# Three edits to a routed attention and bilinear feed-forward kernel: no arithmetic on GpSimd, one PSUM bank of their own for the preparations, sorting scratch in another weight's room

## The chip, the cores and the metric

One core of a Trainium2 chip runs the whole program. The metric is the device time of one execution in microseconds (us); the kernel before was timed three times, and its median is compared. The core has five engines that run their own instruction streams in order and wait for each other by semaphores: PE (TensorE, matrix products), DVE (VectorE), ACT (ScalarE), POOL (GpSimd) and SP (SyncE, which here only starts transfers).

## The reference

```python
# attention: q, k, v are (4 batches, 8 heads, 768 tokens, 64), 16 centroids per head
q_n = q / (norm(q) + 1e-06);  k_n, c_n likewise
q_assign = argmax(einsum('bhsd,hcd->bhsc', q_n, c_n), axis=-1)   # one of 16 clusters
k_assign = argmax(einsum('bhsd,hcd->bhsc', k_n, c_n), axis=-1)
mask = q_assign[:, :, :, None] == k_assign[:, :, None, :]
scores = where(mask, matmul(q, k^T) / 8, -1e9)
attn = softmax(scores);  out = matmul(attn, v)
# feed-forward on x = out as (3072 tokens, 512)
a = x @ w_a;  b = x @ w_b            # 512 -> 1536, float64 inputs, used as float32
y = (a * b) @ w_out                  # 1536 -> 512
```

## The kernel before, in words

**Two ways to do the attention.** Heads are taken in pairs, four pairs to a batch, 16 in all. The first eight pairs (batches 0 and 1) are *dense*: all 768x768 scores of a head are computed, and a one-hot code of the cluster, added as a small bf16 product before the real one (`score`, L590, both), makes a key of another cluster vanish in the exponential. The other eight pairs (numbers n = 1 to 8, batches 2 and 3) are *sorted*: rows of q, k and v are scattered by indirect transfers into lists by cluster (`put`, L1410), each list is reloaded and attended by itself (L1482 to L1526), and results are gathered back (`get`, L1547) and transposed (L1562).

**The dense loop.** It runs over 48 groups of two key blocks. In each group PE computes scores (L590), ACT takes the exponential (L600), PE multiplies the probabilities by v (`weigh`, L636), and DVE adds probabilities up for the softmax denominator (`add_up`, L619; for the first pair POOL does it, L624). Once per half pair PE sums over keys (`denominators`, L655), ACT copies that out (L660), and DVE transposes, inverts and scales (`normalize`, L675 to L689; the scaling of pairs 0 to 2 is POOL's). Between these stand the *preparations* of the next dense pair: for pairs 4 to 7 a transpose on DVE (L503), similarities to the centroids on PE (`prep_sim`, L400), a transpose back (L507), the choice of the best cluster (L528 to L533), the one-hot code (L513, L515), its transpose (L519), and eight small transfers that spread it (L523). The sorted pairs' first steps are preparations too: transposes of the rows (L1249, copied out at L1254), similarities (L1260), and positions in the lists (L1307, L1309).

**The weights.** 36 parts of 128x512 float64 words arrive by transfers into two buffers named `raw` (L299) and are turned into float32 by `round_w`: four instructions on DVE (L310, L313, L317, L320), two on ACT, and a last add of the rest on POOL (L328). Parts 0 to 23 are `w_a` and `w_b`, parts 24 to 35 `w_out`, one for each block of 128 of the 1536 middle features. Eight have fixed places in the dense loop; the others are put in by a planner that runs in Python while the program is written. It keeps a clock of its own for each engine (`Clocked`) and a list of events with due times. It decides only the order: what the chip runs is a fixed list for each engine.

**The feed-forward.** Batch 0 is done in two token halves, each of 24 *pieces* of eight matmuls (`ffn_block`: `piece_a` with `w_a`, copied out by ACT; `piece_b` with `w_b`, multiplied into `h` by DVE, L774). 12 of them fall into the dense loop, one in about two groups. Batches 1 to 3 and all second products (`ffn_downs`) use Strassen's scheme of seven products for eight; DVE makes the differences of operands first (L1004 of `h`, L993 of `w_out`, L820 of x) and adds the products up (L1027). All products of the feed-forward share L715.

**PSUM and SBUF.** PSUM has two double banks for scores (`ps_s`), three single banks (`ps_m`) and one for the attention output (`ps_o`). Before the feed-forward begins, preparations take `ps_m`; from then on the feed-forward owns all three banks in turn (`in_turn`), and `apart()` gives a preparation one of the score tiles. The rows of sorted pairs 1 to 4 wait in the room of `h` of the second token half, their keys and scratch in the room of the first (`early_room`). So the fifth piece of the first half has to come after the last positions of pair 4 (`"after", EARLY`), and the second half's pieces after its last scatter (`"put", EARLY`). `late_room` opens new rooms after that.

Of the kernel before, what the change touches and what calls it, by code (L numbers as in the profile page):

```python
# [11 lines left out]
FP32 = mybir.dt.float32  # L12
# [5 lines left out]
ALU = mybir.AluOpType  # L18
# [139 lines left out]
def short_path(nc, tc, ctx, c, cn, centroids_in, casts, n_far, q, k, v,  # L158
# [22 lines left out]
    G_, Gi = (Clocked(nc.gpsimd, "G", us, *state) for us in (1.1, 1.28))  # L181
# [120 lines left out]
    def round_w(i):  # L302
# [25 lines left out]
        G_.tensor_tensor(out=w, in0=w, in1=rest, op=ALU.add)  # L328
# [282 lines left out]
    def add_up(u):  # L611
        p, hf, j = where(u)
        if j == 0 or j == NJ - 1:
            return
        if j == 1:
            accs[p, hf] = accp.tile([P, 2, HB], FP32, name="acc")
        acc = accs[p, hf]
        if p > 0:
            Vd.tensor_tensor(out=acc, in0=probs[u - 1] if j == 1 else acc,  # L619
                             in1=probs[u], op=ALU.add)  # L620
            added[p, hf] = clocks["V"]
            return
        for a in range(2):
            G_.tensor_tensor(  # L624
                out=acc[:, a, :],
                in0=probs[u - 1][:, a, :] if j == 1 else acc[:, a, :],
                in1=probs[u][:, a, :], op=ALU.add)
        added[p, hf] = clocks["G"]
# [35 lines left out]
    def normalize(p, hf):  # L664
# [21 lines left out]
        def apply():  # L686

            eng = V if p >= HP - 1 else G_
            eng.tensor_tensor(out=x, in0=x, in1=den, op=ALU.mult)  # L689
            unchecked.append((4 * p + 2 * hf + 1, inv))  # L690
# [53 lines left out]
    def ffn_block(b, blk):  # L744
# [14 lines left out]
        def piece_a(f):  # L759
            while blk == 0 and f == NCH and ("after", EARLY) not in done:  # L760
                spend(1.0)
                run_due()
            if f == 0:
                while blk == 1 and ("put", EARLY) not in done:
                    spend(1.0)
                    run_due()
                box["h"] = early[blk].rearrange("p (f t) -> p f t", f=NF)
# [375 lines left out]
    wanted, issued = {}, [0.0]  # L1143
# [80 lines left out]
    def sorted_pair(n, start):  # L1224
# [398 lines left out]
        def run_chain(chain, first=0.0):  # L1623
            at_step = [0]

            def step(t):
# [5 lines left out]
                if not gate() or late and clocks[kind] > now[0] + late or (  # L1632
# [8 lines left out]
                f()  # L1641
                at_step[0] += 1
# [14 lines left out]
    blocks, left = {}, {}  # L1657
# [17 lines left out]
    def ffn_ready(p, hf):  # L1675
# [8 lines left out]
        if hf == 0:  # L1684
            blocks[0] = ffn_block(0, 0)
            ffn.extend(counted(0, blocks[0][0]))
        else:
            ups0, box0 = blocks[0]
            ups, box = ffn_block(0, 1)
            pieces = ups  # L1690
# [17 lines left out]
    PER_GROUP = NCH * HB // 2  # L1708
# [25 lines left out]

    def next_round(t):
# [9 lines left out]
        at(t + 6.0, next_round)  # L1745
# [116 lines left out]
    check_inverses()  # L1862
    while events or len(ffn) > 10:
# [283 lines left out]
```

## Time and profile before

| what | value |
|---|---|
| median of 3 runs (lowest, highest) | 1027.24 us (1027.18, 1029.36) |
| the profiled execution's own time | 1026.05 us |
| its span, first to last instruction | 1024.3 us |
| mean granted TensorE clock | 0.981 |
| PE busy | 973.9 us |
| DVE busy | 612.3 us |
| ACT busy | 281.5 us |
| POOL busy | 375.3 us |

The span is what the trace covers; 1.75 us of the profiled execution lie around it. The dense loop ends near 309 us; from there PE runs the feed-forward with the sorted pairs between its pieces. A busy time is the union of an engine's instructions; the granted clock is the share of full speed at which PE was allowed to run, and a matmul at half of it takes twice as long.

### The profile page before, as it was taken

To read this page: it belongs to the slowest core of one execution; us is meant where nothing else is said; L and a number is where in the kernel's file an instruction comes from. 1 tells how busy PE (TensorE), PEld (TensorE's weight loads), DVE (VectorE), ACT (ScalarE), POOL (GpSimd) and SP (SyncE) were. 2 spreads that over 40 slices of the span, in tenths; PEclk is the share of its full clock that TensorE was granted. 3 is DMA by queue.
4 is the path that set the end of the run, shared out by engine and by line. 5 is a ranking of instruction groups with operands and counts; after the bars stand their busy time and mean duration, and the time that the engine had idled before them with its cause. 6 is when DMAs were issued, how large, how long until landed. Compare 5 with 4: busy or idle time off the path is not lost.

```text
span 1024.3 us, 20493 instructions
## 1 busy us (share of the span) xinstructions
PE 973.9 (95%) x7966; PEld 508.1 (50%) x7966; DVE 612.3 (60%) x1256; ACT 281.5 (27%) x586; POOL 375.3 (37%) x359
## 2 busy tenths in 40 slices
PE   8988958898799999999999999999999999999997
PEld 5443323343344454665554556755454665444564
DVE  5599869779665574767765653755353534333442
ACT  5755635353453331101222210112122001111100
POOL 3515856445564213434454443344443310000000
PEclk9999989999899999999999999999999999999999
DMA  6987455532236654564746277272832302222300
GB/s 184 240 228 164 108 122 151 124 92 79 77 100 169 157 103 100 157 148 108 133 105 150 71 167 184 66 174 82 166 83 66 124 27 73 56 59 62 119 32 30
DMA packets 266776, 118.86 MB, mean 116 GB/s; under 512 B 197552, under 2 KB 252848, under 8 KB 266672
## 3 DMA queue, kind: packets, MB, share of 16 engines
q1 hardware_dynamic: 257040, 104.44, 41.3%
q0 software_dynamic: 9216, 12.60, 4.5%
q8 instruction: 65, 1.06, 0.4%
q10 hardware_dynamic: 416, 0.43, 0.1%
q14 instruction: 39, 0.32, 0.1%
HBM read 79.46 MB, written 37.55 MB: 114 GB/s over the span
## 4 chain that ended last, share of the span: by engine, by line
PE 73%; DVE 3%; SPq 1%; DMA 1%; ACT 1%; issue 1%; DVEq 0%
PE m L715 62%; PE s L590 2%; PE s L1482 2%; PE O L636 2%; PE s L1507 2%; PE s L1516 1%; DMA raw<-down_sums 1%; PE O L1249 1%; PE s L1562 1%; PE s L655 0%; SPq L523 0%; PE O L1260 0%; SPq L1238 0%; SPq L990 0%; SPq L1440 0%
## 5 line engine op out<-in xcount | busy, mean ns | idle before, releaser
L1547 POOL DMA_INDIRECT xT<-od,idx x96 | 93.8, 977 | 123.1 <-PE m L715 118.0
L715 PE MATMUL m<-xT,wa_sb 128*64 128x384 f32 x672 | 116.5, 487 | 0.0
L715 PE MATMUL m<-xT,wb_sb 128*64 128x384 f32 x672 | 116.2, 487 | 0.0
L600 ACT ACTIVATE pt<-s 128x768 f32<-128x768 f32 x96 | 75.2, 809 | 97.3 <-PE s L590 56.8
L892 DVE TENSOR_TENSOR ha<-ha,m 128x384 f32<-128x384 f32 x72 | 39.7, 552 | 95.0 <-PE m L715 71.9
L889 ACT COPY h<-m 128x384 f32<-128x384 f32 x72 | 34.5, 479 | 199.5 <-PE m L715 180.0
L715 PE MATMUL m<-wo_sb,h 128*64 128x256 f32 x768 | 87.3, 380 | 0.0
L892 DVE TENSOR_TENSOR h<-h,m 128x384 f32<-128x384 f32 x72 | 39.7, 551 | 72.4 <-PE m L715 55.4
L715 PE MATMUL m<-raw 128*64 128x384 f32 x432 | 79.1, 487 | 1.0 <-DVE raw L854 1.0
L636 PE MATMUL O<-pt,v 128*64 128x384 f32 x384 | 75.8, 518 | 3.2 <-ACT xT L643 3.2
L590 PE MATMUL s<-qkT 64*128 64x384 f32 x384 | 77.8, 523 | 0.0
L715 PEld LDWEIGHTS m<-xT,wb_sb 128*64 128x64 f32 x672 | 47.8, 137 | 59.1 <-issue 55.1
L715 PEld LDWEIGHTS m<-xT,wa_sb 128*64 128x64 f32 x672 | 47.4, 137 | 58.4 <-issue 53.3
L1410 POOL DMA_INDIRECT qd<-whole,idx x48 | 48.2, 1005 | 68.3 <-PE m L715 53.9
L1410 POOL DMA_INDIRECT kvd<-whole,idx x48 | 48.7, 1014 | 63.0 <-PE m L715 49.8
L1410 POOL DMA_INDIRECT qd<-h,idx x48 | 54.9, 1143 | 44.3 <-PE O L636 24.2
L715 PEld LDWEIGHTS m<-wo_sb,h 128*64 128x64 f32 x768 | 54.6, 137 | 28.4 <-issue 1.4
L715 PE MATMUL m<-xT,h 128*64 128x256 f32 x576 | 64.9, 380 | 0.0
L1410 POOL DMA_INDIRECT kvd<-h,idx x48 | 51.3, 1070 | 26.9 <-PE s L590 14.6
L590 PE MATMUL s<-ohT 64*128 64x384 bf16 x192 | 30.0, 342 | 28.1 <-DMA ohT<-h 15.6
L715 PE MATMUL m<-xT,size 128*64 128x384 f32 x288 | 52.7, 487 | 0.0
L715 PEld LDWEIGHTS m<-xT,h 128*64 128x64 f32 x576 | 40.7, 137 | 20.8 <-DVE h L1004 0.5
(286 smaller groups left out, 1518.1 us busy)
## 6 DMA issues: line engine op xcount, KB each, us to landing
whole<-kvd SPq DMA_DIRECT2D x64, 160.0 KB
raw<-in_moe_w_a_dram SPq DMA_DIRECT2D x12, 512.0 KB
raw<-in_moe_w_b_dram SPq DMA_DIRECT2D x12, 512.0 KB
raw<-in_moe_w_out_dram SPq DMA_DIRECT2D x12, 512.0 KB
raw<-up_sums SPq DMA_DIRECT2D x96, 64.0 KB
kvd<-xT SPq DMA_DIRECT2D x4, 1280.0 KB
whole<-qd SPq DMA_DIRECT2D x32, 160.0 KB
od<-whole SPq DMA_DIRECT2D x32, 160.0 KB
```

The lines of the kernel that those rows point to most:

```text
L590: ins = nc.tensor.matmul(out=s[:, a, 0:HB], lhsT=Ts[p][r, S + j * P:S + (j + 1) * P], rhs=Ts[p][r, hf * HB:(hf + 1) * HB], start=start, st ...
L600: Sl.activation(out=pt, in_=s[:, :, 0:HB], func=AF.Exp, scale=SCALE)
L636: ins = nc.tensor.matmul(out=O_of[0][a * D:(a + 1) * D, 0:HB], lhsT=vs[p][:, a, j, :], rhs=probs[u][:, a, :], start=(j == 0), stop=(j == N ...
L715: ins = nc.tensor.matmul(out=ps[half], lhsT=lhsT[:, half], rhs=rhs, **kw)
L889: S_.copy(out=box[name], in_=box["X"][:, 0:HB])
L892: V.tensor_tensor(out=box[name], in0=box[name], in1=box[bank][:, 0:HB], op=ALU.add)
L1249: nc.tensor.transpose(out=ps[:, x * P:(x + 1) * P], in_=(M["qr"], M["kk"])[w][:, j].rearrange("p a d -> p (a d)"), identity=ident)
L1410: ins = Gi.indirect_dma_start(out=dst[:, :], out_offset=bass.IndirectOffsetOnAxis(ap=M["idx"][:, w, j, a:a + 1], axis=0), in_=src, in_offs ...
L1482: nc.tensor.matmul(out=tiles[s // 2][r0:r0 + m, s % 2, c0:c0 + m], lhsT=M["skT"][r, h, 32 * x:32 * x + m], rhs=M["sqT"][r, h, 32 * x:32 * ...
L1507: nc.tensor.matmul(out=ps[:, s, 65 * i:65 * i + 65], lhsT=pt[:, P * i:P * i + P], rhs=vt[:, i, :], start=True, stop=True)
L1516: nc.tensor.matmul(out=ps[r, s, 65 * (2 + i):65 * (3 + i)], lhsT=pt[r, 2 * P + D * i:2 * P + D * i + D], rhs=vt[r, 2 + i, :], start=True, ...
L1547: paced(Gi.indirect_dma_start(out=M["xs"][:, j, a * D:(a + 1) * D], out_offset=None, in_=od[n][:, :], in_offset=bass.IndirectOffsetOnAxis( ...
```

## The change

POOL loses its three kinds of adds and multiplies, which become DVE instructions. `in_turn` takes two banks in place of three, and the third one, `beside`, is handed to every preparation until `late_room` gives it back to the feed-forward. A gate spaces the preparations of sorted pairs by 0.3 us of planned time. Rows and scratch of sorted pairs 1 to 4 move from the first half's `h` into the room of `w_out` (one of the two row buffers stays in the second half's `h`). With that the waits of the pieces change, and so does their order: 16 pieces of the first half, the second half's blocks 6, 7 and 0 to 5, the rest of the first half, the rest of the second. `PER_GROUP` rises, which lets 15 pieces fall into the dense loop. The rounding of the weights gets new rules: parts 8 to 15 from a date on or when DVE is idle, 16 to 23 when it is idle, and `w_out` only after the last scatter of pair 4. What is left of the rounding is written in one go before the first product of `ffn_downs` (`with_weights`, unchanged).

```diff
@@ round_w
-        G_.tensor_tensor(out=w, in0=w, in1=rest, op=ALU.add)
+        V.tensor_tensor(out=w, in0=w, in1=rest, op=ALU.add)
@@ apart
-    banks = []
+    banks, beside = [], []
     def apart():
+        if beside:
+            return beside[0]
         if banks:
             return ps_s.tile([P, 2, 512], FP32, name="s")[:, 0, :]
@@ add_up
-        if p > 0:
-            Vd.tensor_tensor(out=acc, in0=probs[u - 1] if j == 1 else acc,
-                             in1=probs[u], op=ALU.add)
-            added[p, hf] = clocks["V"]
-            return
-        for a in range(2):
-            G_.tensor_tensor(
-                out=acc[:, a, :],
...
-        added[p, hf] = clocks["G"]
+        Vd.tensor_tensor(out=acc, in0=probs[u - 1] if j == 1 else acc,
+                         in1=probs[u], op=ALU.add)
+        added[p, hf] = clocks["V"]
@@ normalize
-            eng = V if p >= HP - 1 else G_
-            eng.tensor_tensor(out=x, in0=x, in1=den, op=ALU.mult)
+            V.tensor_tensor(out=x, in0=x, in1=den, op=ALU.mult)
@@ in_turn
-            banks.extend(ps_m.tile([P, 512], FP32, name="m") for _ in range(3))
+            banks.extend(ps_m.tile([P, 512], FP32, name="m") for _ in range(2))
+            beside.append(ps_m.tile([P, 512], FP32, name="m"))
@@ piece_a
-            while blk == 0 and f == NCH and ("after", EARLY) not in done:
+            if blk == 0 and f >= NF - 2:
+                assert dense_done
+            while blk == 1 and f < NF // 2 and ("put", EARLY - 1) not in done:
                 spend(1.0)
                 run_due()
-            if f == 0:
-                while blk == 1 and ("put", EARLY) not in done:
-                    spend(1.0)
-                    run_due()
@@ early_room
-        rooms([t[:, 0:ROW], t[:, ROW:2 * ROW]], extra[:, 2 * S:4 * S],
-              early[0][:, 3 * S:], early[0][:, 2 * S:])
+        w = wo_sb.rearrange("p f n -> p (f n)")
...
+        rooms([new(ROW), t[:, 0:ROW]], new(2 * S), new(HB + 512 + 2 * (NJ + 1) * 2 * NC),
+              new(2 * NJ * D))
@@ late_room
         dense.close()
+        banks.append(beside.pop())
@@ run_chain, step
-                if not gate() or late and clocks[kind] > now[0] + late or (
+                if not gate() or kind == "T" and side_at[0] > now[0] or late and (
+                        clocks[kind] > now[0] + late) or (
...
+                if kind == "T":
+                    side_at[0] = last[0] + 0.3
@@ ffn_ready
-            ffn.extend(counted(0, blocks[0][0]))
+            ffn.extend(counted(0, blocks[0][0][:16]))
...
-            pieces = ups
+            part = lambda fs: [x for f in fs for x in ups[2 * f:2 * f + 2]]
+            pieces = part((6, 7, 0, 1, 2, 3, 4, 5)) + later[16:] + part((8, 9, 10, 11))
@@ the dense loop and the rounding
-    PER_GROUP = NCH * HB // 2
+    PER_GROUP = NCH * HB * 5 // 8
...
+    def may_round(i):
+        idle = clocks["V"] <= now[0] + 0.6
+        if i < 16:
+            return idle or now[0] > ROUND + 9.0 * (i - 8)
+        if i < 24:
+            return idle and now[0] > 240 or ("put", EARLY) in done
+        return idle and was("put", EARLY, 4)
+
+    ROUND = 122.0
...
-        if not (i in raws and arrived[i] + 4.5 <= now[0] and clocks["V"] <= now[0] + 1.0):
+        if not (i in raws and arrived[i] + 4.5 <= now[0] and may_round(i)):
             at(now[0] + 0.5, next_round)
...
-        at(t + 6.0, next_round)
+        at(max(t + 3.5, now[0]), next_round)
```

More of the change, by code (lines that the diff above doesn't have):

```diff
@@ L1142, in short_path @@
     busy = []
-    wanted, issued = {}, [0.0]
+    wanted, issued, side_at = {}, [0.0], [0.0]
     ROW = 2 * NJ * 3 * D
@@ L1176, in early_room, with new @@
         early.append(t)
-        rooms([t[:, 0:ROW], t[:, ROW:2 * ROW]], extra[:, 2 * S:4 * S],
-              early[0][:, 3 * S:], early[0][:, 2 * S:])
+        w = wo_sb.rearrange("p f n -> p (f n)")
+        at_ = [0]
+        def new(n):
+            at_[0] += n
+            return w[:, at_[0] - n:at_[0]]
+        rooms([new(ROW), t[:, 0:ROW]], new(2 * S), new(HB + 512 + 2 * (NJ + 1) * 2 * NC),
+              new(2 * NJ * D))
     def late_room():
         dense.close()
+        banks.append(beside.pop())
         post = ctx.enter_context(tc.tile_pool(name="post", bufs=1))
@@ L1655, in n_stat @@
         return slice(c0, c0 + 1)
-    blocks, left = {}, {}
+    blocks, left, dense_done = {}, {}, []
     def counted(b, pieces):
```

9 lines of the change are left out of this document (4 added, 5 removed).

## The prediction

> **What bounds the kernel now.** I read the page first, then the busy times by stage, then what PE waits for in the stages where it idles.
>
> ```profile
> span 1024.3 us, 20493 instructions
> ```
> ```profile
> 52.00:134.00 82.00, 67.60 (x444) 30.93 (x440) 73.02 (x131) 44.56 (x86) 44.57 (x33) 0.95 0.63 154
> 134.00:140.00 6.00, 1.12 (x6) 0.73 (x8) 4.16 (x7) 0.00 (x0) 2.10 (x2) 0.50 0.15 44
> 140.00:265.00 125.00, 108.56 (x644) 46.91 (x642) 102.67 (x176) 56.17 (x109) 67.78 (x59) 0.94 0.48 115
> 265.00:309.00 44.00, 41.41 (x239) 18.59 (x241) 27.37 (x45) 22.39 (x47) 27.80 (x25) 0.92 0.33 106
> 309.00:407.00 98.00, 98.00 (x775) 46.63 (x773) 54.86 (x109) 28.24 (x63) 25.43 (x24) 1.00 0.62 134
> 407.00:1024.00 617.00, 608.83 (x5525) 338.51 (x5521) 321.62 (x722) 97.40 (x223) 183.38 (x185) 1.00 0.40 102
> ```
>
> The windows give, after the length, the busy time of PE, PEld, DVE, ACT and POOL, then the granted clock. From 309 us on PE idles 8.2 us in 715: that part is bound by PE, and the change leaves PE its products. So what can be won lies in the dense loop: 14.4 us idle in 52 to 134, 4.9 in the next 6, and 16.4 + 2.6 = 19.0 from 140 to 309. What can be lost is a new gap after 309. DVE is nearly as full as PE in the loop: 73.02 of 82.
>
> The table of waits for PE, 140 to 309 us, names the owner of those 19.0:
>
> ```profile
> PE s L590 <- ACT acc L660: 5.8, 8, 2.1
> PE s L590 <- DMA ohT<-h: 4.2, 4, 2.1
> PE s L590 <- ACT xT L1254: 3.1, 4, 1.6
> PE s L400 <- ACT pt L600: 2.1, 1, 2.1
> PE s L400 <- DVE qkT L503: 1.6, 1, 1.6
> PE s L590 <- DVE sim L507: 0.7, 2, 0.4
> PE s L1307 <- DVE sim L507: 0.7, 1, 0.7
> ```
>
> The lines with L660, L1254, L600 and L507 are one thing: a preparation sits in a score tile, so that scores wait for it, or it for the exponential. They make 12.4 us. The other waits come from DVE: one-hot codes (4.2) and a transpose (1.6).
>
> Before 140 us the timeline shows the largest gap, and the waits of DVE a reason:
>
> ```profile
> 136.78 0.50 PE L590 MATMUL s<-ohT 64*128 64x384 bf16 x1 [9.24 <-DMA ohT<-h]
> 139.38 0.82 PE L590 MATMUL s<-ohT 64*128 64x384 bf16 x3 [2.10 <-DMA ohT<-h]
> 139.67 2.96 PE L590 MATMUL s<-qkT 64*128 64x384 f32 x8
> ...
> 146.92 1.45 PE L590 MATMUL s<-qkT 64*128 64x384 f32 x8
> ```
> ```profile
> DVE rest L317 <- POOL wa_sb L328: 2.8, 1, 2.8
> DVE acc L619 <- POOL xT L689: 0.9, 1, 0.9
> ```
>
> PE stood 9.24 + 2.10 = 11.3 us for pair 4's one-hot code, and its next scores took 2.96 in place of 1.45 us, since the clock was at 0.50. DVE, which makes that code, stood 3.7 us behind POOL.
>
> **Step 1: POOL's arithmetic on DVE.** What did it cost where it was?
>
> ```profile
> 153.51 2.91 DVE L619 TENSOR_TENSOR acc<-acc,pt 128x768 f32<-128x768 f32 x2
> 153.69 1.92 POOL L328 TENSOR_TENSOR wa_sb<-wa_sb,rest 128x512 f32<-128x512 f32 x1 [1.56 <-DVE rest L320]
> 196.01 1.94 DVE L619 TENSOR_TENSOR acc<-acc,pt 128x768 f32<-128x768 f32 x2
> ```
> ```profile
> L689 DVE TENSOR_TENSOR xT<-xT,acc 128x384 f32<-128x384 f32 x10 | 6.3, 634 | 0.3
> L993 DVE TENSOR_TENSOR xT<-wo_sb 128x512 f32<-128x512 f32 x12 | 7.6, 685 | 0.0
> ```
>
> Two adds of DVE take 1.94 us alone and 2.91 while POOL adds beside them: one POOL add can cost DVE 0.97 us. The same add on DVE costs 0.69 (row L993). In the changed program's order 22 of the 36 round-off adds stand before the last dense denominator (25 in the old one): 22 x 0.69 = 15.2 us. Eight adds of the first pair at 0.97 make 7.8, six scalings at 0.63 make 3.8. DVE takes on 26.8 us. It sheds up to 0.97 for each of the 25 + 6 POOL operations that ran beside a busy DVE, and the 3.7 of waiting; where POOL ran beside an idle DVE it sheds nothing. So the step is worth between +26.8 and 26.8 - 31 x 0.97 - 3.7 = -7.0 on DVE. I take zero in sum, nearer to the second, since most of those adds fell where DVE was over 80% busy; and 7.8 of the 26.8 lie before 52 us, with idle time on DVE to hide them.
>
> The Trainium skill, "Perfetto Trace Analysis", section "Optimizing Scalar/DVE Operations", speaks against the step: with a saturated DVE it may make sense to move work to GPSIMD, though the port that the two share may undo it. By its first half this step would add its 26.8 us to an engine that is 73.02 of 82 busy; the pair 2.91 and 1.94 bears out the second.
>
> How pair 4's code moves: between 52 us and that code DVE loses 3.7 us of waits and one whole rounding (nine stand ahead of it before, eight after), whose price is four rows:
>
> ```profile
> L320 DVE SCALAR_TENSOR_TENSOR rest<-raw,rest 128x512 f32<-128x512 uint32 x11 | 7.6, 693 | 0.4
> L313 DVE SCALAR_TENSOR_TENSOR wo_sb<-raw,wo_sb 128x512 int32<-128x512 int32 x11 | 7.6, 693 | 0.4
> L310 DVE TENSOR_SCALAR wo_sb<-raw 128x512 int32<-128x512 int32 x11 | 5.5, 498 | 0.0
> L317 DVE TENSOR_SCALAR rest<-wo_sb 128x512 int32<-128x512 int32 x11 | 4.7, 427 | 1.2
> ```
>
> That is 2.3 us; with the 0.69 that follows, a rounding is now 3.0. The adds there trade 5 x 0.69 + 5 x 0.63 = 6.6 against 11 x 0.97 = 10.7 at most. The code comes 6 to 10 us earlier, I take 8; the 11.3 us gap shrinks by 8.0 and the slow scores regain 2.96 - 1.45 = 1.5. Term A: -9.5 us, between -12.8 (all of it) and -3.7 (the waits alone).
>
> **Step 2: the bank beside.** Of the 19.0 us idle after 140 the 12.4 of shared tiles go. New waits come, because preparations now queue behind each other in one bank. Example: pair 5's similarities hold it until DVE's L507, which stands behind an add and a rounding (0.97 + 3.0 + 0.6 = 4.6 us), while PE has a piece (2.7 us) to do before the next denominator wants the bank: 1 to 2 us. Other such pairs wait for an ACT copy; I count 3 us in all, between 0 and 6. Of the 4.2 + 1.6 that hang on DVE I take 2 back. The clock at 0.94 and 0.92 costs at most 0.06 x 125 + 0.08 x 44 = 11.0 us of full-speed time; with fewer gaps I take 4. That makes 12.4 - 3 + 2 + 4 = 15.4; but DVE is left with almost no slack against PE, so I take 12. Term B: -12 us, between -20 and 0. The three more pieces in the loop win nothing by themselves, since PE has to do them anyway.
>
> **Step 3: two banks for pieces.** In the loop a piece comes once in a group or two, and the bank is long free. From the loop's end to `late_room` pieces stand back to back, and the bank of a `piece_b` must be emptied by DVE (0.55 us) within the 2.7 us of the next piece. At most one rounding of 3.0 us stands between two such reads, against 5.4 us from one to the next. +1 us, between 0 and 3.
>
> **Step 4: the scratch in `w_out`'s room.** The pieces need not wait for pair 4, but the rounding of `w_out` does. In the order before, all 36 roundings end some ten pieces ahead of the first second product. After, three of them (parts 33, 34, 35) stand directly behind the last `h` and ahead of the differences (L1004, L993). The second product, `"12"` by `"21"`, needs `w_out` blocks 6 to 11, and the load of part 35 cannot start before part 33 has been read, for there are two `raw` buffers. Prices:
>
> ```profile
> 409.40 2.74 PE m L715 x24
> ```
> ```profile
> 138.84 0.53 SPq L299 DMA_DIRECT2D raw<-in_moe_w_b_dram  x1
> 142.60 0.43 DVE L310 TENSOR_SCALAR wb_sb<-raw 128x512 int32<-128x512 int32 x1 [4.24 <-DMA raw<-in_moe_w_b_dram]
> ```
> ```profile
> L1004 DVE TENSOR_TENSOR ha<-h 128x384 f32<-128x384 f32 x32 | 16.3, 552 | 0.0
> ```
>
> Let the last piece end at 0. DVE: `h` until 0.6, part 33 read until 2.9, done 3.6; part 34 done 6.6; part 35, issued at 3.0, lands 3.8 later at 6.8 and is done at 9.8. PE: first product until 2.7, then 10 of 12 blocks of the second, 2.3 us, until 5.0; with 9.8 for the last block it stands 4.8. Next, S1 and T1 need four L1004 (2.2) and one L993 (0.7): 12.7, while PE is back at 10.3: 2.4 more. T1, T2 and S2 end at 17.1, the product before at 15.4, and its first block needs S2's first half at 16.6: 1.2 more. 8.4 us, in a stage where PE idled none. After gaps like this the clock halves, as at 139.67: I add 2. Term C: +10.4 us, between 0 (the roundings run ahead) and 14 (a transfer late by 3.5). The Trainium skill, "TensorE: Matmul & The Clock Gate", Part 1, has the clock halve after an idle window of about 3.4 us and return after a busy one; by that the addition is an estimated 0 to 3.4 us, depending on where the windows lie.
>
> **Step 5: the sorted pairs come later.** In PE's order the fifth pair's rows are transposed behind 34 pieces, before behind 28, and the last transposition (L1562), which had 9 pieces' worth of products behind it, now stands right at the end of batch 2's, where batch 3 starts.
>
> ```profile
> 838.42 0.81 PE s L1562 x6
> 839.23 173.26 PE m L715 x1272
> ```
> ```profile
> L1564 ACT COPY xT<-s 128x768 f32<-128x768 f32 x8 | 6.4, 799 | 6.2 <-PE s L1562 5.8 <-DMA qd<-whole,idx 0.3
> L820 DVE TENSOR_TENSOR raw<-xT 128x384 f32<-128x384 f32 x12 | 6.4, 551 | 0.2
> ```
>
> After it stood 173 us of products without a wait. Now the copy (0.8) and six differences (6 x 0.55 = 3.3) have only two products of 1.4 us beside them: 4.1 - 2.8 = 1.3, so +1.5 us, between 0 and 4.
>
> **Sum.** -9.5 - 12 + 1 + 10.4 + 1.5 = -8.6 on 1026.05: 1017.4 us for the profiled execution. The median of before is 1.2 above it, so 1018.6.
>
> **The rivals.** (a) *DVE becomes the bound of the loop.* POOL's adds did not hold DVE up as much as 0.97 each, or DVE, without slack, passes the banks' gain on as waits for one-hot codes and denominators. Then A is -3.7, B 0 or worse, and the gap of step 4 is paid out of nothing: -3.7 + 1 + 10.4 + 1.5 = +9.2, 1036.4 us: slower. For it: 73.02 of 82. The Trainium skill's "Perfetto Trace Analysis", in the section named above, points this way. Against it: the stretched adds and the 12.4 us that are no wait for DVE. It decides when DVE's busy time from 52 to 309 us, 207.2 before, grows by over some 10 us. Chance 0.18. (b) *No gap at the second products*, because PE is slowed elsewhere or the roundings run ahead of it: C is 0, 1008.2 us. Against it: the order is fixed, and part 35's load must follow part 33. Chance 0.12. (c) *The bank only renames waits*: B is -3, which leaves +0.4: 1027.6, no change. Chance 0.10. That the change doesn't do what it says is ruled out by the order: POOL keeps only transfers and set-up.
>
> **How the numbers follow.** My forecast has 0.60, with 1010 to 1025 as its own range. The range 1006 to 1033 leaves out the worse half of (a) and the best of (b). A measurement tells 0.2% (2.1 us) from no change. Faster: 0.60 + 0.12 = 0.72; same 0.05; slower 0.18 and half of (c), 0.23.
>
> **What would show it.** Right: the wait for `ohT` near 130 us is under 5 us; L660, L1254 and L600 vanish from the waits of L590; L619 averages near 0.95 us; DVE stays near 207 us in the loop; PE has a gap of 7 to 10 us in front of L715 on `wo_sb`, released by DVE. Wrong: a loop as long as before with DVE over 90% busy, or no gap at the second products.

## The result, and the profile after

The changed kernel takes 1013.38 us (median of 4 runs, 1012.14 to 1013.56), the kernel before 1028.3 us beside it (4 runs). The ratio is 0.9852, 95% interval 0.9835 to 0.9869: faster by 14.9 us, inside the predicted range, 5.2 us under the predicted 1018.6. The profiled execution took 1013.33 us, its mean clock was 0.984.

The page of the changed kernel gives the span, the busy times, and the granted clock in 40 slices of 25.3 us:

```profile
span 1011.6 us, 20445 instructions
...
PE 969.7 (96%) x7966; PEld 508.1 (50%) x7966; DVE 626.3 (62%) x1306; ACT 280.2 (28%) x586; POOL 299.1 (30%) x301
...
PEclk9999989999999997999999999999999999999999
```

The sixth slice (126 to 152 us) shows a lowered clock, and so does the sixteenth, from 379 to 405 us. The busy times by stage (length, then PE, PEld, DVE, ACT, POOL, then the clock):

```profile
52.00:134.00 82.00, 69.62 (x454) 32.95 (x452) 76.92 (x147) 44.34 (x86) 27.15 (x24) 0.95 0.65 159
134.00:140.00 6.00, 6.00 (x36) 2.31 (x35) 5.86 (x10) 2.77 (x6) 2.73 (x3) 0.89 1.24 253
140.00:265.00 125.00, 113.87 (x716) 49.72 (x714) 95.00 (x174) 54.09 (x104) 52.86 (x49) 0.96 0.40 93
265.00:309.00 44.00, 43.11 (x270) 18.75 (x268) 32.54 (x57) 22.18 (x51) 20.46 (x20) 1.00 0.43 124
309.00:407.00 98.00, 91.92 (x751) 45.51 (x749) 70.14 (x136) 27.91 (x62) 8.89 (x9) 0.95 0.71 148
407.00:1012.00 605.00, 596.97 (x5411) 333.19 (x5407) 311.54 (x703) 96.16 (x221) 184.11 (x185) 1.00 0.41 102
```

From 52 to 309 us PE idles 24.4 us where it idled 38.3 (the four lengths less the four busy times). DVE is busy 76.92 + 5.86 + 95.00 + 32.54 = 210.3 us there, 207.2 before. From 309 to 407 PE, which idled none, idles 6.1 us, at a clock of 0.95.

The ends of stages can be read off the order of PE's products. The dense loop, up to the last product of its last denominator, ends at 293.4 us (308.0 before) and holds three pieces, 8.1 us, more: 14.6 + 8.1 = 22.7 us won. The last piece of batch 0 ends at 384.0 (406.2): 22.2 won. Batch 0's second products take 75.4 us (65.0): 10.4 given back. From there to the last product it is 545.7 us (546.8). So -22.2 + 10.4 - 1.1 = -12.9, against -12.7 between the two profiled times.

What PE waits for from 140 to 309 us, by the changed kernel's own line numbers (scores are L592, `weigh` L630, `prep_sim` L402, the feed-forward L709); columns are total, times, longest:

```profile
PE m L402 <- ACT wo_sb L1315: 3.2, 1, 3.2
PE s L592 <- DMA ohT<-h: 2.9, 2, 1.5
PE s L592 <- ACT pt L602: 2.5, 1, 2.5
PE m L1249 <- ACT wo_sb L1254: 2.5, 3, 1.1
PE O L630 <- ACT xT L637: 0.9, 1, 0.9
```

Scores no longer wait for a preparation in their tile: the lines with L660, L1254 and L507 of before have no counterpart in front of L592, and one wait for an exponential is left. In their place stand waits of one preparation for another in the one bank: 3.2 + 2.5 = 5.7 us. And the adds for the denominator, on DVE, of the kernel before and then of the changed one (count, busy us, mean ns):

```profile
L619 DVE TENSOR_TENSOR acc<-acc,pt 128x768 f32<-128x768 f32 x42 | 46.9, 1117 | 1.4
```
```profile
L620 DVE TENSOR_TENSOR acc<-acc,pt 128x768 f32<-128x768 f32 x48 | 45.5, 948 | 1.9 <-ACT pt L602 0.3
```

### The profile page after: what moved, and what is told of

Same layout as the page of the kernel before. It is cut to its first block, busy times and chain, and to the rows that moved or that the text cites. A ratio compares the mean times of both kernels' runs of the same rounds, so it can differ in the third digit from the quotient of the medians.

```text
span 1011.6 us, 20445 instructions
## 1 busy us (share of the span) xinstructions
PE 969.7 (96%) x7966; PEld 508.1 (50%) x7966; DVE 626.3 (62%) x1306; ACT 280.2 (28%) x586; POOL 299.1 (30%) x301
## 4 chain that ended last, share of the span: by engine, by line
PE 85%; DVE 11%; DMA 1%; ACT 1%; issue 1%; SPq 1%; DVEq 0%; ACTq 0%
PE m L709 65%; PE s L592 5%; PE O L630 4%; PE s L1482 2%; PE s L1507 2%; DVE acc L620 2%; PE s L1516 1%; PE m L649 1%; PE m L402 1%; SPq L525 1%; PE O L1249 1%; PE s L1562 1%; DVE rest L320 1%; PE m L1249 1%; DMA raw<-up_sums 1%
## 5 line engine op out<-in xcount | busy, mean ns | idle before, releaser
L709 PE MATMUL m<-xT,wb_sb 128*64 128x384 f32 x672 | 116.2, 487 | 0.0
L709 PE MATMUL m<-xT,wa_sb 128*64 128x384 f32 x672 | 116.1, 487 | 0.1
L709 PE MATMUL m<-wo_sb,h 128*64 128x256 f32 x768 | 88.0, 382 | 4.7 <-DVE wo_sb L328 4.7
L709 PE MATMUL m<-raw 128*64 128x384 f32 x432 | 79.6, 488 | 1.0 <-DMA raw<-up_sums 0.8
L709 PEld LDWEIGHTS m<-xT,wa_sb 128*64 128x64 f32 x672 | 48.1, 137 | 59.1 <-issue 51.8
L709 PEld LDWEIGHTS m<-xT,wb_sb 128*64 128x64 f32 x672 | 47.8, 137 | 58.2 <-issue 51.6
L592 PE MATMUL s<-qkT 64*128 64x384 f32 x384 | 75.1, 509 | 0.0
L630 PE MATMUL O<-pt,v 128*64 128x384 f32 x384 | 73.7, 507 | 1.1 <-ACT xT L637 1.1
L709 PEld LDWEIGHTS m<-wo_sb,h 128*64 128x64 f32 x768 | 54.5, 137 | 34.2 <-DVE wo_sb L328 5.9
L709 PE MATMUL m<-xT,h 128*64 128x256 f32 x576 | 67.4, 391 | 1.4 <-DVE xT L985 1.4
L1410 POOL DMA_INDIRECT qd<-h,idx x24 | 27.2, 1133 | 108.8 <-DMA qk<-in_q_dram 75.4
L709 PEld LDWEIGHTS m<-xT,h 128*64 128x64 f32 x576 | 42.1, 141 | 24.3 <-DVE xT L985 2.6
L709 PE MATMUL m<-xT,size 128*64 128x384 f32 x288 | 52.8, 487 | 0.0
L709 PEld LDWEIGHTS m<-raw 128*64 128x64 f32 x432 | 30.9, 137 | 37.3 <-issue 31.0
L881 ACT COPY ha<-m 128x384 f32<-128x384 f32 x54 | 25.9, 479 | 79.4 <-PE m L709 77.8
```

Of the source, the lines that this page charges most:

```text
L592: ins = nc.tensor.matmul(out=s[:, a, 0:HB], lhsT=Ts[p][r, S + j * P:S + (j + 1) * P], rhs=Ts[p][r, hf * HB:(hf + 1) * HB], start=start, st ...
L630: ins = nc.tensor.matmul(out=O_of[0][a * D:(a + 1) * D, 0:HB], lhsT=vs[p][:, a, j, :], rhs=probs[u][:, a, :], start=(j == 0), stop=(j == N ...
L709: ins = nc.tensor.matmul(out=ps[half], lhsT=lhsT[:, half], rhs=rhs, **kw)
L881: S_.copy(out=box[name], in_=box["X"][:, 0:HB])
L1410: ins = Gi.indirect_dma_start(out=dst[:, :], out_offset=bass.IndirectOffsetOnAxis(ap=M["idx"][:, w, j, a:a + 1], axis=0), in_=src, in_offs ...
```

## The experiments

Twelve kernels ran in three groups. The group of e1 to e4 ran on a chip on which the kernel before took 1039.36 us, so kernels are compared by their ratio to the kernel before on the same chip. The changed kernel did not run on that chip. There the time behind batch 0's second products is 553.1 us in e1 and e2 (both the changed kernel but for one part) and 559.8 and 558.1 in e3 and e4 (both the kernel before but for one part), where the chip of the first result has 545.7 and 546.8 for the two kernels themselves. So some 5 us, half a per cent, can lie between chips in a comparison of e1 or e2 with 0.9852, and the intervals do not hold that. "Pieces done" is the time at which batch 0's last piece ends in the profiled execution; it does not depend on how many pieces fall into the loop. "Ahead of codes" is how many of the 36 weight parts DVE has rounded ahead of each of the four one-hot codes.

| kernel | median us | ratio, 95% interval | loop ends | pieces done | ahead of codes |
|---|---|---|---|---|---|
| before | 1027.24 | 1 | 308.0 | 406.2 | 9, 14, 15, 19 |
| changed | 1013.38 | 0.9852 (0.9835 to 0.9869) | 293.4 | 384.0 | 8, 12, 16, 16 |
| e1 changed, POOL adds back | 1025.44 | 0.9881 (0.9854 to 0.9908) | 294.8 | 385.8 | 8, 12, 16, 16 |
| e2 changed, no bank beside | 1028.92 | 0.9916 (0.9888 to 0.9944) | 299.6 | 390.2 | 8, 12, 16, 16 |
| e3 old order, DVE adds | 1038.31 | 0.9982 (0.9958 to 1.0006) | 306.4 | 404.6 | 9, 14, 15, 19 |
| e4 old order, bank | 1034.44 | 0.9966 (0.9945 to 0.9986) | 303.9 | 402.1 | 9, 14, 15, 19 |
| e5 changed, again | 1013.38 | 0.9855 (0.9838 to 0.9872) | 294.7 | 385.3 | 8, 12, 16, 16 |
| e6 changed, `w_out` spread | 1005.97 | 0.9783 (0.9766 to 0.9799) | 294.0 | 384.6 | 8, 12, 16, 16 |
| e7 changed, old rounding rule | 1015.70 | 0.9880 (0.9863 to 0.9896) | 305.7 | 396.3 | 8, 12, 15, 17 |
| e8 before, denser pieces | 1029.05 | 1.0014 (1.0005 to 1.0024) | 319.2 | 409.7 | 9, 14, 16, 22 |
| e9 before, new rounding rule | 1023.72 | 0.9961 (0.9944 to 0.9979) | 299.7 | 406.0 | 9, 13, 15, 16 |
| e10 before, DVE + bank + rule | 1015.99 | 0.9890 (0.9860 to 0.9920) | 290.7 | 392.8 | 8, 12, 15, 16 |
| e11 before, DVE + bank | 1006.15 | 0.9786 (0.9759 to 0.9814) | 289.9 | 388.1 | 8, 11, 13, 16 |
| e12 old order, DVE + bank | 1020.43 | 0.9914 (0.9884 to 0.9944) | 307.0 | 405.2 | 9, 14, 15, 19 |

The profiled execution of e12 was the longest of its five (1024.90 us), that of e7 the longest of its four (1018.83, the others 1015.50 to 1015.89), that of e10 the shortest of its five (1010.83), so their times of stages are not typical by some 3 to 5 us; the ratios are.

### One part undone or done, with the order of instructions kept (e1 to e4, e12)

In e1 the add of the rounding goes back to POOL, in the changed kernel's order. The bare name lets the planner charge the engine as before, and the line behind it issues the instruction.

```diff
-        V.tensor_tensor(out=w, in0=w, in1=rest, op=ALU.add)
+        V.tensor_tensor
+        nc.gpsimd.tensor_tensor(out=w, in0=w, in1=rest, op=ALU.add)
```

> The changed kernel with the last add of each weight's rounding back on POOL; the planner is charged as before, so every engine's order is that of the changed kernel. Theory (POOL's adds cost DVE as much as they save, and make it wait): in the dense loop 22 adds of 0.69 us leave DVE and up to 0.97 us of stretch comes back for each, plus waits for POOL of some 4 us; the three roundings in one go ahead of the second products get longer too, by 0.6 us each. So 3 to 10 us slower than the changed kernel, about 1019 us, and L620 averages 1.05 us or more again. Rival (only the order of the pieces and the roundings counts, the engine of an add does not): within 2 us of the changed kernel, 1012 to 1015 us.

By the ratio e1 is 0.29% slower, at the lower edge of the theory's 3 to 10 us, and the two intervals overlap. The sign that the theory named is there: DVE's adds are stretched again, to 1076 ns from 948:

```profile
L621 DVE TENSOR_TENSOR acc<-acc,pt 128x768 f32<-128x768 f32 x48 | 51.7, 1076 | 1.7
```

But the loop ended at 294.8 us, and the changed kernel's own two profiles have 293.4 and 294.7 (e5), so it lost nothing there that can be told. The gaps at the second products grew, since the adds of the last three parts now take longer (waits of PE in e1, second products):

```profile
PE m L710 <- POOL wo_sb L329: 6.3, 3, 3.2
```

So in this order the engine of the rounding's add alone is worth little.

In e2 the changed kernel loses the bank and keeps everything else.

```diff
-        if beside:
-            return beside[0]
...
-            banks.extend(ps_m.tile([P, 512], FP32, name="m") for _ in range(2))
-            beside.append(ps_m.tile([P, 512], FP32, name="m"))
+            banks.extend(ps_m.tile([P, 512], FP32, name="m") for _ in range(3))
...
-        banks.append(beside.pop())
```

> The changed kernel with preparations in the score tiles again and three banks for the pieces, orders as in the changed kernel. Theory (shared score tiles cost 12.4 us of waits in the loop, less 3 for the new bank's own): 7 to 13 us slower, about 1023 us, and L592 waits again for L654 or L662-like copies of denominators and transposes. Rival (c) of the prediction (the bank only renames waits): within 3 us, 1011 to 1016 us.

The loop ended 6.2 us later than the changed kernel's first profile and 4.9 later than its second (e5), across chips; the ratio is 0.64% higher, its interval apart. That lies between the theory's 7 to 13 us and the rival's 3. The waits of PE in e2, 140 to 309 us, are again those of shared tiles:

```profile
PE s L590 <- ACT acc L652: 4.6, 8, 0.9
PE s L400 <- ACT pt L600: 2.6, 1, 2.6
```

In e3 the kernel before issues POOL's three kinds of arithmetic on DVE at the same places, with the planner charged as before:

```diff
-        G_.tensor_tensor(out=w, in0=w, in1=rest, op=ALU.add)
+        G_.tensor_tensor
+        nc.vector.tensor_tensor(out=w, in0=w, in1=rest, op=ALU.add)
...
-            eng.tensor_tensor(out=x, in0=x, in1=den, op=ALU.mult)
+            (V if p >= HP - 1 else G_).tensor_tensor
+            nc.vector.tensor_tensor(out=x, in0=x, in1=den, op=ALU.mult)
```

and likewise in `add_up`. In e4 it gets the bank and keeps POOL's arithmetic; e12 has both.

```diff
+        if beside:
+            return beside[0]
...
-            banks.extend(ps_m.tile([P, 512], FP32, name="m") for _ in range(3))
+            banks.extend(ps_m.tile([P, 512], FP32, name="m") for _ in range(2))
+            beside.append(ps_m.tile([P, 512], FP32, name="m"))
...
+        banks.append(beside.pop())
```

> The kernel before, in its own order, with POOL's three kinds of adds and multiplies issued on DVE (the planner is still charged for POOL). Theory: the 3.7 us of DVE's waits for POOL and the stretch go, 26.8 us of work comes; pair 4's one-hot code is earlier by 5 to 8 us: 1017 to 1023 us. Rival (a) (a full DVE becomes the bound of the loop): 1029 to 1037 us, slower than before.

> The kernel before, in its own order, with the bank beside and two banks for the pieces. Theory: 12.4 us of waits go, up to 6 come: 1015 to 1023 us. Rival (c): 1025 to 1029 us, no change, because DVE holds the loop.

> The kernel before with its order of instructions kept, POOL's arithmetic issued by DVE at the same places, and the bank beside. Alone in that order the adds gave 1.6 us of the loop and the bank 4.1. If the two are independent the loop ends 5 to 6.5 us earlier than 308.0, ratio 0.994 to 0.996; if they help each other (with neither a shared tile nor POOL in its way DVE gets ahead) over 9 us, ratio under 0.992; if they cost each other (DVE without slack passes the bank's gain on as other waits) under 3.5 us, ratio over 0.997.

The ratios are 0.9982, 0.9966 and 0.9914: -0.2%, -0.3% and, together, -0.9% (0.6 to 1.2%). The two parts alone add up to -0.5%, within the interval's reach of the -0.9%, so a help of one for the other is suggested and not shown. e3 and e4 both gained less than their theories had it (0.4% at least). In neither e3 nor e12 was DVE's added work a loss, and in none of the three did the loop gain the 20 us that the prediction had given the two parts.

### The two parts with a new order (e11), and the rounding rule (e7, e9, e10)

In e7 the changed kernel gets back the old rule for when parts 8 to 23 are rounded; as a side effect its `w_out` parts spread too.

```diff
         if i < 16:
-            return idle or now[0] > ROUND + 9.0 * (i - 8)
+            return clocks["V"] <= now[0] + 1.0
         if i < 24:
-            return idle and now[0] > 240 or ("put", EARLY) in done
+            return clocks["V"] <= now[0] + 1.0
...
-        at(max(t + 3.5, now[0]), next_round)
+        at(t + 6.0, next_round)
```

> The changed kernel with the old rule for when parts 8 to 23 are rounded (DVE at most 1.0 us behind, every 6 us). As a side effect the last three parts of w_out are spread as in e6, so the second products are no test here; the dense loop is. Theory R (the new dates of the roundings, which keep DVE free for the one-hot codes, are what shortened the loop): it ends 6 to 12 us later than the changed kernel's, and the transposes of the one-hot codes (L519 before, L521 after) come later by as much. Theory D (three more pieces in PE's gaps shortened it): it ends within 2 us of the changed kernel's, and the whole is 6 to 10 us faster by the spread.

The loop of e7 ended 11.0 us later than that of e5 beside it. By the medians e7 is only 2.3 us slower, but its second products take 7.0 us less, so the rule is worth some 9 us. This made me suspect that the rounding rule, which the prediction had not priced, was the largest part of the gain ("theory R"). Waits of PE in e7, 140 to 309 us:

```profile
PE s L592 <- ACT pt L602: 5.2, 1, 5.2
PE m L402 <- ACT wo_sb L1315: 4.6, 1, 4.6
PE m L1260 <- ACT wo_sb L1254: 3.7, 1, 3.7
```

None of the three is a wait for a one-hot code. From 52 to 309 us PE waits 9.5 us for codes (`ohT`) in e7 and as much in e5, so theory R's reason, that the new dates keep DVE free for the codes, does not hold. What grew are the waits for the exponential (8.2 us, 4.8 in e5) and for the one bank (10.3, 5.7 in e5). Nor did the codes come later by as much: the four transposes start 1.8 us earlier, 4.1, 3.7 and 11.6 later than in e5.

Three kernels built up from before test it. e9 has the rule alone:

```diff
+    def may_round(i):
...
-        if not (i in raws and arrived[i] + 4.5 <= now[0] and clocks["V"] <= now[0] + 1.0):
+        if not (i in raws and arrived[i] + 4.5 <= now[0] and may_round(i)):
...
-        at(t + 6.0, next_round)
+        at(max(t + 3.5, now[0]), next_round)
```

Its `may_round` is that of the change, but for the last twelve parts, which it lets through when DVE is idle. e11 has POOL's arithmetic on DVE and the bank beside, with the old rule, written as in the change, so that the planner counts the adds on DVE's clock and lays the instructions anew:

```diff
-        G_.tensor_tensor(out=w, in0=w, in1=rest, op=ALU.add)
+        V.tensor_tensor(out=w, in0=w, in1=rest, op=ALU.add)
...
-            eng = V if p >= HP - 1 else G_
+            eng = V
```

and `add_up` and the bank as in the change's diff. e10 is e11 with the rule of e9. None has the new rooms, piece order or density.

> The kernel before with one part of the change: the new rules for when a part of the weights is rounded (parts 8 to 15 from a date on or when DVE is idle, 16 to 23 when it is idle, the later ones when idle, the next one looked at 3.5 us after the last). POOL keeps its arithmetic, the three banks, the rooms and the piece order stay as they were. Theory R, that the dates of the roundings are the largest part of the loop's gain (undoing them in the changed kernel cost 11.0 us of its loop): the loop ends 7 to 11 us earlier than before's 308.0, the ratio is 0.989 to 0.993. Rival, that the dates only pay once POOL no longer holds DVE up and the preparations have their bank: the loop ends within 3 us of 308, ratio 0.997 to 1.003. The prediction gave the dates no term of their own, beyond one rounding of 2.3 us ahead of pair 4's code.

> The kernel before with two parts: POOL's arithmetic on DVE (counted there by the planner) and the bank beside; the roundings by the old rule. The prediction's terms A and B together were 21.5 us, and steps 1 and 2 are all that is in this kernel: by it the loop ends about 20 us earlier than 308, ratio near 0.980. Theory R: 1.6 for the adds and 4 to 6 for the bank, so 5 to 8 us, ratio 0.992 to 0.996, and the difference between this kernel and the one with the dates as well is 7 to 12 us of the loop.

> The kernel before with three parts together: POOL's arithmetic on DVE (the planner counts it there), the bank beside, and the new dates of the roundings. Rooms, piece order and density of pieces as before. Theory, that these three make the loop's gain and the rest makes none: the loop ends 14 to 22 us earlier than 308 (the changed kernel's own 14.6 hold three pieces, 8.1 us, more), ratio 0.980 to 0.987. Rival, that moving the scratch and the order of the pieces free the loop too: under 12 us, ratio over 0.988. A gap of at most 2 us at the second products, since w_out can be rounded early here.

Theory R fell. e9 ends its loop 8.3 us earlier, as the theory had it, but has its pieces done no earlier (406.0 against 406.2), and its ratio of 0.9961 lies between the theory's range and the rival's: the roundings left out of the loop make PE wait for a weight behind it (timeline of PE in e9: start, length, instruction, idle before):

```profile
312.56 1.54 PE L715 MATMUL m<-xT,wa_sb 128*64 128x384 f32 x4 [5.72 <-POOL wa_sb L328]
```

e11, with the two parts alone and the old rule, is at 0.9786, 20.9 us under before: nearly all of the forecast -21.5 of terms A and B, 18.1 of it by the end of the loop. e10, with the rule on top, is at 0.9890: slower than e11, and over its forecast of 0.980 to 0.987 although its loop ends 17.3 us earlier than before's. Even in its fastest execution, the profiled one, it ends the loop 0.8 us and the pieces 4.7 us later than e11. So the rule is worth some 9 us in the changed kernel's order and costs time in e11's; it has no price of its own.

e11 against e12 is the same pair of edits, with the order laid anew and with the order kept: 0.9786 against 0.9914, intervals apart. One thing that differs shows in front of pair 4's one-hot code. The timeline of DVE (start, length), in before, with the POOL add that runs beside, then in e12, then in e11:

```profile
129.75 0.43 DVE L317 TENSOR_SCALAR rest<-wb_sb 128x512 int32<-128x512 int32 x1 [2.84 <-POOL wa_sb L328]
...
131.50 1.52 DVE L515 TENSOR_TENSOR h<-sim,first 64x384 bf16<-64x384 f32 x1
133.06 0.58 DVE L519 STREAM_TRANSPOSE h<-h 128x384 bf16<-128x384 bf16 x1
```
```profile
127.45 0.97 POOL L1410 DMA_INDIRECT qd<-h,idx  x1 [0.30 <-issue]
128.44 1.27 POOL L328 TENSOR_TENSOR wa_sb<-wa_sb,rest 128x512 f32<-128x512 f32 x1
130.98 1.63 POOL L328 TENSOR_TENSOR wb_sb<-wb_sb,rest 128x512 f32<-128x512 f32 x1 [1.27 <-DVE rest L320]
```
```profile
125.31 0.69 DVE L329 TENSOR_TENSOR wa_sb<-wa_sb,rest 128x512 f32<-128x512 f32 x1
...
128.29 0.69 DVE L329 TENSOR_TENSOR wb_sb<-wb_sb,rest 128x512 f32<-128x512 f32 x1
...
129.56 0.55 DVE L518 TENSOR_TENSOR h<-sim,first 64x384 bf16<-64x384 f32 x1
130.15 0.58 DVE L522 STREAM_TRANSPOSE h<-h 128x384 bf16<-128x384 bf16 x1
```
```profile
122.86 0.69 DVE L328 TENSOR_TENSOR wb_sb<-wb_sb,rest 128x512 f32<-128x512 f32 x1
...
125.32 0.58 DVE L521 STREAM_TRANSPOSE h<-h 128x384 bf16<-128x384 bf16 x1
```

DVE stood 2.84 us in before because POOL's add stood behind a scatter on POOL, and both roundings share the tile `rest`. Two roundings stand in front of the code in before and in e12, one in e11. Taking POOL away, with the bank, wins 2.9 us (133.06 to 130.15; 2.6 without the bank, in e3), the new order 4.8 more. At the fourth code three fewer roundings stand ahead (19 and 16 in the table). That code is done at 244.4 us in e11 and at 261.6 in e12; three roundings of 3.0 us are 9 of these 17.2 (in the profiled executions). The planner rounds when its own DVE clock is free; with the adds counted on that clock it is free less often, which would put roundings behind the codes.

The codes are the smaller part of it, though. The waits of PE from 52 to 309 us, in e12 and then in e11:

```profile
PE s L593 <- DMA ohT<-h: 19.4, 7, 7.0
PE m L657 <- ACT xT L1258: 3.9, 1, 3.9
PE m L403 <- ACT h L1319: 3.5, 1, 3.5
...
PE O L638 <- ACT xT L645: 2.6, 1, 2.6
```
```profile
PE s L592 <- DMA ohT<-h: 15.2, 5, 4.6
...
PE m L1245 <- ACT xT L1250: 0.7, 1, 0.7
PE m L649 <- ACT xT L1250: 0.7, 1, 0.7
```

PE idles 38.1 us there in e12 and 27.3 in e11. Of these 10.8 us, 4.2 are waits for codes; 7.4 are waits for a copy out of the one bank (3.9, 3.5 and two more of 1.4 in sum, against 0.7 + 0.7), and 2.4 are waits for the attention's output bank (2.6 against 0.2); others are 3 us longer in e11. The rest of the 17.1 us between the two loops' ends goes with the clock, 0.91 in e12 and 0.97 in e11 over this stretch, and e12's profiled execution was a long one. Fewer roundings do not make codes earlier by themselves either: e9 has no more of them ahead of the second and third code than before, and has these codes later (done at 180.0 and 218.7 us, against 174.9 and 213.2).

### The second products and the density (e5, e6, e8)

e5 is the changed kernel again, beside e6 and e7. e6 lets the planner round the last twelve parts earlier:

```diff
-        return idle and was("put", EARLY, 4)
+        return clocks["V"] <= now[0] + 1.0 and was("put", EARLY, 2)
```

> The changed kernel once more, as the base of the other three runs, which share its chip. Ratio to the kernel before as at first, 0.983 to 0.987; the three roundings in front of the second products leave PE about 6 us of waits (L709 on wo_sb and on xT).

> The changed kernel with another condition for the roundings of w_out: DVE may be 1.0 us behind (was 0.6), and they may start 2 us after the last scatter of pair 4 (was 4). In the planner's order the last three then stand apart from each other, and only part 35 is left for the moment before the second products. Theory (term C: the roundings in one go cost 8 us of idle time and some clock): PE's waits there fall from 6 us to 2 or less, the clock does not fall, and the time is 7 to 11 us under the changed kernel's. Rival (the gap is hidden: the sorted pairs or DVE would have stopped PE there anyway, or later): within 2 us of the changed kernel.

In the changed kernel, PE then DVE at the second products:

```profile
383.88 4.53 PE L709 MATMUL m<-wo_sb,h 128*64 128x256 f32 x40
390.80 0.65 PE L709 MATMUL m<-wo_sb,h 128*64 128x256 f32 x4 [2.40 <-DVE wo_sb L328]
393.78 1.12 PE L709 MATMUL m<-wo_sb,h 128*64 128x256 f32 x4 [2.32 <-DVE wo_sb L328]
396.25 6.94 PE L709 MATMUL m<-xT,h 128*64 128x256 f32 x38 [1.36 <-DVE xT L985]
```
```profile
390.06 0.69 DVE L328 TENSOR_TENSOR wo_sb<-wo_sb,rest 128x512 f32<-128x512 f32 x1
390.67 0.42 DVE L310 TENSOR_SCALAR wo_sb<-raw 128x512 int32<-128x512 int32 x1
...
393.03 0.69 DVE L328 TENSOR_TENSOR wo_sb<-wo_sb,rest 128x512 f32<-128x512 f32 x1
```

And PE in e6:

```profile
384.47 5.40 PE L709 MATMUL m<-wo_sb,h 128*64 128x256 f32 x48
391.69 2.81 PE L709 MATMUL m<-xT,h 128*64 128x256 f32 x24 [1.82 <-DVE xT L985]
395.26 2.81 PE L709 MATMUL m<-xT,h 128*64 128x256 f32 x24 [0.76 <-DVE h L996]
```

The waits for the three last parts are gone, only the operands' differences are waited for, and the clock holds (24 products in 2.81 us, where 38 took 6.94). e6 is 7.4 us faster than the changed kernel beside it; batch 0's second products take 68.3 us for 75.4. e6 (1005.97) and e11 (1006.15) are the fastest kernels of the study, and beat both kernels that were compared.

e8 is the kernel before with the new `PER_GROUP`, which puts three more pieces into the loop.

> The kernel before with PER_GROUP of the changed one, so that 15 pieces and not 12 fall into the dense loop; nothing else. Theory D: the loop ends at most 1 us later than the old one's although it holds 8 us more of products, and the whole is 6 to 9 us faster than before. Theory R: the loop ends 5 to 9 us later and the whole is within 3 us of before. By the prediction, which gave the pieces nothing, it is within 2 us of before.

Its loop ended 11.2 us later and held 8.1 us more products; its pieces were done 3.5 us later than before, and the ratio is 1.0014 (1.0005 to 1.0024). In this order density gives nothing, as the prediction had it. A single wait of PE stands out in e8's loop: 6.8 us of the similarities (L400) for a transpose on DVE (L503).

## Why the prediction was right, and where its working was not

**The sums held.** For the loop it had -9.5 - 12 + 1 = -20.5 us, measured -22.7; for the second products +10.4, measured +10.4; for what comes after +1.5, measured -1.1. The total, -8.6, was 4.1 us short of the profiled -12.7. The two edits to which A and B belong bring -20.9 us by themselves (e11), and the whole change without the late roundings brings the same (e6, 0.9783 against 0.9786): rooms, piece order, density and rounding rule together neither win nor lose measurably beyond term C. Stage by stage the two differ: e6 has its pieces done 3.5 us before e11 and spends 3.8 more behind them.

**Step 1 had the code's time right, for a partly wrong reason, and made too much of it.** Pair 4's code was to come 8 us earlier and came 7.5 earlier (its transpose at 125.57, from 133.06). Term A added to that time a clock regained, and this is what PE did there in the changed kernel:

```profile
129.36 0.50 PE L592 MATMUL s<-ohT 64*128 64x384 bf16 x1 [4.58 <-DMA ohT<-h]
131.90 0.82 PE L592 MATMUL s<-ohT 64*128 64x384 bf16 x3 [2.03 <-DMA ohT<-h]
132.19 3.08 PE L592 MATMUL s<-qkT 64*128 64x384 f32 x8
```

The gap was to shrink by 8.0 and shrank by 4.7, from 11.3 to 6.6, because PE came to it 2.8 us earlier too. The slow scores were to regain 1.5 us and regained nothing: 3.08 us, at a clock of 0.50 from 128.5 to 135.3. They end 7.4 us earlier than before (135.27 for 142.63), where term A has 9.5.

DVE's sum was to be zero: its busy time in the loop went from 207.2 to 210.3 us (211.0 in e12, which keeps the order of before), and the adds fell from 1117 to 948 ns. So rival (a), to be decided at 10 us more on DVE, is refuted, and e3 shows it directly: in the old order the work moved to DVE costs nothing (0.9982). The Trainium skill's "Perfetto Trace Analysis", section "Optimizing Scalar/DVE Operations", holds here by its second half, the shared port (1117 ns against 948), and not by the first. But the larger part of the code's 7.5 us is not POOL's removal, which won 2.9 with the order kept: it came with the new order, 3.0 us of it as the one rounding that the planner no longer places ahead of this code, and which the prediction had. What the new order does at the three later codes (2 roundings fewer, 1 more, 3 fewer) and in the bank was not looked up, though it could be read in the order.

**Step 2 is the step that failed in its working.** It had 12.4 us of waits that go with the bank, 3 of new ones, 2 back from DVE, and 4 of clock, and took 12 of the 15.4. Measured: PE's idle time from 140 to 309 us went from 19.0 to 12.0, so 7.0 and not 11.4; new waits in the one bank are 5.7 us and not 3. The bank by itself is worth 5 to 6 us of the loop (e2) or 0.34%, 3.5 us, in the old order (e4): mis-sized, though inside its range of -20 to 0. The clock made up for it: 0.96 and 1.00 in the two stages for 0.94 and 0.92, which is 0.02 x 125 + 0.08 x 44 = 6.0 us where 4 were taken. Idle time and clock make 13.0 for the 12: that the errors cancel is luck. Rival (c), that the bank only renames waits and leaves B at -3, has e2 against it in the changed kernel's order; in the old order e4's 3.5 us are about what it says. That A and B together came out is luck in part as well: kept in before's order the two edits bring 0.9% (e12), and only the order that the planner makes of them brings 2.1% (e11), for which the prediction had no term beyond one rounding.

**Step 3** took 1 us for two banks. PE has no wait at all from 293 to 384 us in the changed kernel, and e4, with the bank alone, takes as long from the loop's end to the last piece as before (98.2 us): the two banks cost nothing.

**Step 4 was right in its mechanism and nearly in its parts.** Counted from the last piece's end at 384.0, part 34 was to be done at 6.6 and part 35 at 9.8; they are done at 6.7 and 9.7, and part 35's load delays nobody (DVE goes from 390.06 to 390.67 without a wait). PE stands 2.40 + 2.32 = 4.7 us for the two, forecast 4.8; 1.36 for the next operands, forecast 2.4; and none for the third, forecast 1.2. Idle was 6.1 us of the forecast 8.4, which fits PE itself running at half speed there. The clock was to take 2 us:

```profile
391.40:401.60 10.20, 6.52 (x32) 3.37 (x32) 8.97 (x17) 1.31 (x4) 1.24 (x1) 0.50 0.74 169
```

6.52 us of products at 0.50 lose 3.3. By the Trainium skill's "TensorE: Matmul & The Clock Gate", Part 1, this was estimated at 0 to 3.4, and the measured loss is at the upper end; but the idle window of about 3.4 us, after which that page has the clock halve, is not in this trace, whose longest gap here is 2.40. Idle and clock make 9.4 of the 10.4; e6 wins back 7.4 and keeps 2.6 of idle time. Rival (b) is refuted.

**Step 5** forecast 1.5 us at batch 3's start. In the changed kernel the products follow the last transposition at once:

```profile
841.01 0.88 PE L1562 MATMUL s<-ident,xT 128*128 128x128 f32 x6
841.81 2.80 PE L709 MATMUL m<-xT,wa_sb 128*64 128x384 f32 x16
```

**What stays open.** Why the old rounding rule costs the changed kernel some 9 us (e7), and the new one costs e10 time, was not settled beyond this: in e7 it is not the codes but the one bank, the exponential and the clock, and both change the order at many places at once. That laying the order anew makes the difference between e12 and e11 is shown; by which of its many moves is not. The roundings ahead of the codes can be counted, but PE's waits give the codes 4.2 us and the banks 9.8, and no run moved one without the other.

## What to carry to other kernels

Where a planner lays out the order, price an edit in the order that it makes, not in the order of the trace: the same two edits were worth 0.9% in the old order and 2.1% in the new one, because charging the work to the busy engine moves everything else that the planner places. Here roundings moved behind the codes and preparations met less often in their one bank; how much each is worth was not separated. Undoing one part in the changed kernel does not give its worth either, when parts act through the order; build up from the kernel before as well. And look at what a moved piece of work leaves to be done in one go: three roundings behind the last piece cost 7.4 us, and one line that spreads them won it back.

## What the runs showed of the hardware

**Several short gaps in a row halved the clock.** None of the gaps at the second products is longer than 2.40 us, and 0.65 us of products stand between the first two; still the clock was at 0.50 for 10.2 us from 391.4 on. In e2 the same three gaps (2.41, 2.33 and 1.36 us) cost 6.8 us at 0.50, so their length alone does not fix the loss. The two gaps of e6, 1.82 and 0.76 us with 2.81 us of products between, left it at full speed.

**What a POOL add cost DVE was not the POOL add's own length.** Two adds of 1.94 us took 2.91 beside one POOL add (in the prediction); a 64x384 bf16 operation that takes 0.55 in e12 (L518) took 1.52 beside one in before (L515). Both are 0.97 us longer, while the POOL adds themselves are shown with 1.92 and 1.63. It is no fixed price: an integer instruction of the rounding (L310) that takes 0.42 us took 0.92 and 0.77 in before beside two other POOL adds of 1.27 and 1.29.

**Chips differ.** The kernel before took 1027.03 to 1028.30 us (medians of three groups) and, on the chip of e1 to e4, 1039.36, over 1% more, with the same program. The loop is not where it is lost: e3 ends its loop and its pieces earlier than before does on the other chip, and takes 13 us more behind the second products (559.8 for 546.8).
